# Sliding-window attention and a squared-ReLU FFN on one core: the first block's casts and copies are dealt out anew, w_in is read in 2 KB rows, more pieces get staging homes, and the first stores are issued later

## The chip, the core and the metric

The kernel runs on one core of a Trainium2 chip. The metric is the device time of one execution in microseconds; the time before is the median of three runs. In this text PE is TensorE, DVE is VectorE, ACT is ScalarE, POOL is GpSimd, and SP is SyncE, which only issues DMAs here.

## What is computed

Eight batches of causal attention with a window of 64 positions, 8 heads of 64, 576 positions; then an FFN over all 4608 tokens.

```python
batch, n_heads, seq, head_dim = (8, 8, 576, 64)
rel = pos[:, None] - pos[None, :]
mask = (rel >= 0) & (rel < 64)
attn = softmax(where(mask, q @ k.T / sqrt(64), -1e9))       # per batch and head
x = (attn @ v).transpose(0, 2, 1, 3).reshape(4608, 512)
h = np.maximum(x @ w_in, 0.0)                               # w_in 512 x 2048
out = (h * h) @ w_out                                       # w_out 2048 x 512
```

## The kernel before

The tokens are worked on in nine blocks of 512: block g below 8 is the first 512 positions of batch g, and the ninth collects the last 64 positions of all batches. In the code g0, g1, g2, g3 are the first four. A block's 8 heads are four pairs `hp`. All matrix work is in fp16; the inputs are fp32 and come in by DMA as 256 KB pieces of 128x512 (`load_qk_pair`, `load_v_pair` for the first three blocks, `load_part` from block 3 on).

The steps of one block are small functions. `cast_qk_pair` and `cast_v_pair` turn a piece to fp16; `shift_v_pair` writes v once more, moved by 64 rows (`v_od`), in two halves. `T` transposes q and k of a pair on PE (eight 128x128 transposes) and copies them from PSUM. `add_mask` puts the mask into PSUM with two matmuls, `Sc` adds the scores (16 small matmuls) and takes the exponential on ACT. `AV` multiplies with v, `N` normalises on DVE, `X` transposes the result on PE and copies it into `xT`. `F1` is x @ w_in for 128 hidden columns (four matmuls over c, L358), then ReLU on DVE (L361) and the square on ACT (L362); `F1_open` (L374) does the first of the four matmuls early. `F2` is the second product in quarters (L394), scaled on ACT into `osb`, of which there are five buffers. From block 1's F2 on, products of sums of weights and of activations (`T_sum` into `wsum`, `S_sum` into `hsum`) replace part of the matmuls. `busy` issues matmuls whose result nobody reads.

The order of the instructions on every engine is written out by hand (`tc.manual_schedule()`), and each engine works its own list in order; a step waits only for its operands and for the buffer that it writes. SP issues nearly all DMAs in program order, each one waiting for the DMA eight before it. From block 3 on the q and k of a block are transposed by DMAs on SP (`transpose_part`), four for q and four for k, each behind POOL's cast. The 9 blocks are staggered: while block g's F2 runs, block g+1's F1 and block g+2's attention are woven in.

Staging: a loaded fp32 piece lies in one of ten `stp` buffers unless `homes` names a place for it. `hsum` and `wsum` are 8 places of 128x512 fp32 each; they first hold v of block 0, w_in and w_out, then (hsum) the first eight pieces of block 2, and later the sums. The list `to_store` collects output stores; they are issued on SP when the next F2 reaches its quarter 1.

w_in is loaded as eight pieces of 512 KB. In the first four each row read is 256 columns, 1 KB, and a piece holds all four c of these columns; in the last four a row is 512 columns, 2 KB, and a piece holds two c. POOL casts each piece in two casts.

Of the kernel before, what the change touches and what calls it, by code (L numbers as in the profile page):

```python
# [8 lines left out]
FP32 = mybir.dt.float32  # L9
FP16 = mybir.dt.float16  # L10
AF = mybir.ActivationFunctionType
# [4 lines left out]
def kernel(  # L16
# [17 lines left out]
    P = 128  # L34
# [81 lines left out]
    def copy(engine, out, in_):  # L116
        if engine is nc.scalar:
            engine.activation(out=out, in_=in_, func=AF.Copy, scale=1.0)  # L118
        else:
            engine.tensor_copy(out=out, in_=in_)  # L120
# [3 lines left out]
    w_out_sb = const.tile([P, FFC, DM], FP16, name="w_out_sb")  # L124

    def load_w_in(i):
        if i < 2:
            if i == 0:
                st["w_in"] = h2pool.tile([P, 4, DMC, 256], FP32, name="w_st", tag="h2")
            for half in range(2):  # L130
                cols = slice(i * 512 + half * 256, i * 512 + half * 256 + 256)
                nc.sync.dma_start(
                    out=st["w_in"][:, 2 * i + half, :, :],
                    in_=moe_w_in[:, cols].rearrange("(c p) f -> p c f", p=P))
            return
        for c in range(0, DMC, 2):
            to = wsum[:, 4 * (i - 2) + c:4 * (i - 2) + c + 2, :]
            st["w_in", i, c], st["w_in", i, c + 1] = to[:, 0, :], to[:, 1, :]
            nc.sync.dma_start(
                out=to, in_=moe_w_in[c * P:(c + 2) * P, i * 512:(i + 1) * 512].rearrange("(c p) f -> p c f", p=P))  # L140

    def cast_w_in(i, c, engine):
        if i < 2:
            half, c = c // 2, 2 * (c % 2)
            copy(engine, w_in_sb[:, c:c + 2, i * 512 + half * 256:i * 512 + half * 256 + 256],
                 st["w_in"][:, 2 * i + half, c:c + 2, :])
            return
        copy(engine, w_in_sb[:, c, i * 512:(i + 1) * 512], st["w_in", i, c][:])

    def load_w_out(f):  # L150
# [33 lines left out]
    def cast_qk_pair(g, what, hp, engine):  # L184
        t = p16p.tile([P, 512], FP16, name=f"{what}16", tag=f"{what}16")
        p16[what, g, hp] = t
        copy(engine, t[:].rearrange("p (i h d) -> p h i d", i=4, h=2),
             st[what, g, hp][:].rearrange("p (h i d) -> p h i d", i=4, h=2))

    def cast_v_pair(g, hp, engine):  # L190
        copy(engine, ev[g, 0][:, :, pair(hp), 0:D].rearrange("p c h d -> p h c d"),
             st["v", g, hp][:].rearrange("p (h c d) -> p h c d", h=2, c=4))
# [55 lines left out]
    def T(g, hp, pool=ps_tr, tag="tr", engine=nc.scalar, own=None):  # L248

        qkt = apool.tile([P, 2, 512], FP16, name="qk", tag="qk")  # L250
        if own is not None:
            tr = at_ps[own][:, 0, :].bitcast(FP16).rearrange("p (a b) -> p a b", a=2)
        else:
            tr = pool.tile([P, 2, 512], FP16, name="tr", tag=tag)
        for a, what in enumerate("qk"):
            for i in range(4):
                nc.tensor.transpose(out=tr[:, a, i * P:(i + 1) * P],  # L257
                                    in_=p16[what, g, hp][:, i * P:(i + 1) * P], identity=ident[:])
        copy(engine, qkt[:].rearrange("r a (p i) -> r a p i", i=4),
             tr[:].rearrange("r a (i p) -> r a p i", i=4))  # L260
        qT[g, hp, "unit"], kT[g, hp, "unit"] = qkt[:, 0, :], qkt[:, 1, :]
# [3 lines left out]
    def add_mask(g, hp, apart=False, i=0):  # L265

        if apart:
            sc = [ps_f1.tile([P, 512], FP32, name="sc1", tag="f1")[:] for _ in range(2)]
        else:
            sc = [at_ps[i][:, hh, :] for hh in range(2)]  # L270
        added[g, hp] = sc
        for hh in range(2):
            nc.tensor.matmul(sc[hh], ident[:], maskb[:, 0, :], start=True, stop=False)
# [116 lines left out]
    def F2(g, ts, quarter, pool, tag, into=None):  # L390
        if quarter == 0:
            f2[g, ts] = into if into is not None else pool.tile([P, 512], FP32, name="ops", tag=tag)
        for f in range(4 * quarter, 4 * quarter + 4):
            nc.tensor.matmul(f2[g, ts][:], h2[g][:, f, ts * P:(ts + 1) * P], w_out_sb[:, f, :],  # L394
                             start=(f == 0), stop=(f == FFC - 1))
        if quarter == 3:
            osb = opool.tile([P, DM], FP32, name="osb", tag="osb", bufs=5)
            nc.scalar.activation(out=osb[:], in_=f2[g, ts][:], func=AF.Copy, scale=OUT_SCALE)
            to_store.append(lambda: store(g, ts, osb))
        if quarter == 1:  # L400
            while to_store:
                to_store.pop(0)()

# [215 lines left out]
    with tc.manual_schedule():  # L619
# [7 lines left out]
        for hp in range(HP):  # L627
# [2 lines left out]
                load_v_pair(g0, 0)  # L630
            load_qk_pair(g0, "q", hp)
            load_qk_pair(g0, "k", hp, nc.scalar)
        nc.scalar.activation(out=warm[:], in_=warm[:], func=AF.Exp)
        for hp in range(1, HP):
            load_v_pair(g0, hp)
        for i in range(4):
# [2 lines left out]

        new_v(g0)  # L640
        dve, pool, act = nc.vector, nc.gpsimd, nc.scalar
        for hp in range(3):
            cast_qk_pair(g0, "q", hp, dve)
            cast_qk_pair(g0, "k", hp, dve)
        cast_v_pair(g0, 0, pool)
        cast_qk_pair(g0, "q", 3, pool)
        busy(24, wide=False)
        T(g0, 0)
        busy(1)
        add_mask(g0, 0)  # L650
        Sc(g0, 0)
        T(g0, 1)
        busy(1)
        add_mask(g0, 1, i=1)
        T(g0, 2, ps_f1, "f1", engine=dve)
        cast_qk_pair(g0, "k", 3, dve)
        Sc(g0, 1, i=1)
        add_mask(g0, 2)
        busy(1)
        Sc(g0, 2)  # L660
        T(g0, 3, engine=dve)
        for hp in range(HP):
            shift_v_pair(g0, hp)
        cast_v_pair(g0, 1, act)
        busy(3)
        add_mask(g0, 3, True)
        AV(g0, 0)
        N(g0, 0)
        Sc(g0, 3, True)
        for hp in range(2, HP):  # L670
            cast_v_pair(g0, hp, act)
        busy(1)
        AV(g0, 1, 0)
        N(g0, 1)
        X(g0, 0)
        busy(2)
        AV(g0, 2)
        N(g0, 2)
        X(g0, 1, act, ps_f2, "f2")
        AV(g0, 3, 0)  # L680
        N(g0, 3)
# [44 lines left out]
                cast_v_pair(g1, hp, nc.gpsimd)  # L726
            shift_v_pair(g1, hp, parts=(0, 1) if hp < 3 else (0,))
        new_v(g2)
        for i, key in enumerate([(w, g2, hp) for hp in range(HP) for w in "qkv"][:8]):
            homes[key] = hsum[:, i, :]  # L730
        for hp in range(HP):
            load_qk_pair(g2, "q", hp)
            load_qk_pair(g2, "k", hp)
# [35 lines left out]
        def A(g, hp, i=1):  # L769
            AV(g, hp, i)  # L770
            N(g, hp)
# [11 lines left out]
        cast_v_pair(g1, 2, nc.scalar); cast_v_pair(g1, 3, nc.scalar)  # L783
        shift_v_pair(g1, 3, nc.scalar, (1,))
        A(g1, 0, 0); F(1, second); M(g1, 3)
        A(g1, 1, 1); F(1, second)
        A(g1, 2, 0); X(g1, 0); A(g1, 3, 1); F(1, second)
        X(g1, 1, nc.scalar, *in_f1); X(g1, 2, nc.vector)
        for f in range(2):
            F1_open(g1, f, *(in_f1, in_f2)[f], upto=2)  # L790
        for f in range(2):
            F1_open(g1, f)
        X(g1, 3, nc.vector, *in_f1); T(g2, 0)
        for _ in range(8):
            next_part()
        F(3, first)
# [129 lines left out]
```

## The time and the profile before

| | us |
|---|---|
| median of 3 runs (295.95 to 297.1) | 296.46 |
| the profiled execution's own time | 295.8 |
| its span in the profile | 294.1 |
| PE busy | 285.6 |
| DVE busy | 224.7 |
| ACT busy | 177.6 |
| POOL busy | 125.2 |

Busy times are sums over the span; an engine that waits for a semaphore is idle. The profile covers one execution of the program, and its times are counted from the start of the span. HBM read is 38.80 MB and written 9.44 MB. A line number names the line of the kernel before; L118 and L120 are the helper `copy` (ACT, and DVE or POOL), so there the tile tells which step it is.

### The profile page before, as it was taken

To read this page: it belongs to the slowest core of one execution; us is meant where nothing else is said; L and a number is where in the kernel's file an instruction comes from. 1 tells how busy PE (TensorE), PEld (TensorE's weight loads), DVE (VectorE), ACT (ScalarE), POOL (GpSimd) and SP (SyncE) were. 2 spreads that over 40 slices of the span, in tenths; PEclk is the share of its full clock that TensorE was granted. 3 is DMA by queue.
4 is the path that set the end of the run, shared out by engine and by line. 5 is a ranking of instruction groups with operands and counts; after the bars stand their busy time and mean duration, and the time that the engine had idled before them with its cause. 6 is when DMAs were issued, how large, how long until landed. Compare 5 with 4: busy or idle time off the path is not lost.

```text
span 294.1 us, 7511 instructions
## 1 busy us (share of the span) xinstructions
PE 285.6 (97%) x2953; PEld 185.0 (63%) x2953; DVE 224.7 (76%) x395; ACT 177.6 (60%) x308; POOL 125.2 (43%) x215
## 2 busy tenths in 40 slices
PE   6999999999999999999999999999999999999994
PEld 4544445555445466667666766666666666888883
DVE  5677629498866887878769877887798889878781
ACT  3767747688366556565665566556564655587821
POOL 4769739953384347239526632913333000000002
PEclk9999999999999999999999999999999999999999
DMA  7999999999999997999899999899997023202025
GB/s 236 314 333 393 406 276 272 309 202 185 161 260 179 185 215 148 205 185 238 170 193 212 223 184 234 169 192 210 206 215 203 2 38 92 92 1 74 0 74 143
DMA packets 143651, 56.07 MB, mean 191 GB/s; under 512 B 127712, under 2 KB 136160, under 8 KB 143616
## 3 DMA queue, kind: packets, MB, share of 16 engines
q1 hardware_dynamic: 142144, 53.95, 86.1%
q10 hardware_dynamic: 1328, 1.25, 1.3%
q0 software_dynamic: 144, 0.39, 0.6%
q8 instruction: 23, 0.38, 0.6%
q14 instruction: 12, 0.10, 0.1%
HBM read 38.80 MB, written 9.44 MB: 164 GB/s over the span
## 4 chain that ended last, share of the span: by engine, by line
PE 93%; ACT 3%; DMA 1%; DVE 1%; issue 0%; ACTq 0%; DVEq 0%
PE hps L358 37%; PE chain L446 14%; PE side L446 12%; PE ops L394 5%; PE at L318 4%; PE at L288 4%; PE at L480 4%; PE side L394 2%; PE chain L394 2%; PE more L446 2%; PE at L344 2%; DMA st_k<-in_k_dram 1%; PE at L446 1%; PE tr L257 1%; ACT qk L118 1%; PE hps L374 1%
## 5 line engine op out<-in xcount | busy, mean ns | idle before, releaser
L362 ACT ACTIVATE h<-hr 128x512 f16<-128x512 f32 x128 | 80.0, 630 | 78.9 <-DVE hr L361 78.4
L358 PE MATMUL hps<-xT,w_in_sb 128*128 128x512 f16 x496 | 122.4, 379 | 0.2
L361 DVE TENSOR_SCALAR hr<-hps 128x512 f32<-128x512 f32 x127 | 85.8, 686 | 31.0 <-PE hps L358 28.5
L358 PEld LDWEIGHTS <-w_in_sb 128*128 128x128 f16 x500 | 46.7, 98 | 42.4 <-issue 1.4
L446 PEld LDWEIGHTS <-hsum 128*128 128x128 f16 x448 | 43.0, 98 | 11.8 <-DVE hsum L422 0.2
L120 POOL CAST v_ev<-st_v 128x512 f16<-128x512 f32 x31 | 22.6, 730 | 42.9 <-DMA st_v<-in_v_dram 42.9
L446 PEld LDWEIGHTS <-h 128*128 128x128 f16 x336 | 32.6, 98 | 8.4 <-issue 0.4
L120 POOL CAST k<-st_k 128x512 f16<-128x512 f32 x33 | 21.0, 638 | 37.8 <-DMA st_k<-in_k_dram 36.3
L295 ACT ACTIVATE pm<-at 128x1024 f16<-128x1024 f32 x35 | 34.1, 1014 | 1.4 <-PE at L288 1.3
L387 POOL DMA_DIRECT2D out_dram<-osb x3 | 1.8, 594 | 63.4 <-ACT osb L562 62.0
L302 DVE TENSOR_TENSOR pm<-pm,mask 128x1024 f16<-128x1024 f16 x32 | 24.5, 775 | 2.1 <-ACT pm L295 2.1
L328 DVE TENSOR_TENSOR xs<-at,rden 128x512 f16<-128x512 f32 x36 | 24.9, 692 | 1.2
L446 PE MATMUL chain<-wsum,hsum 128*128 128x256 f16 x192 | 24.9, 273 | 0.0
L422 DVE TENSOR_TENSOR hsum<-h 128x1024 f16<-128x1024 f16 x28 | 20.9, 747 | 5.1 <-ACT h L362 5.0
L233 POOL CAST v_od<-st_v 64x512 f16<-64x512 f32 x30 | 22.2, 742 | 1.6
L120 POOL CAST q<-st_q 128x512 f16<-128x512 f32 x28 | 18.7, 692 | 6.5 <-DMA st_q<-in_q_dram 3.1
L394 PEld LDWEIGHTS <-h 128*128 128x128 f16 x128 | 11.5, 97 | 12.2
L318 PEld LDWEIGHTS <-pm 128*64 128x64 f16 x576 | 11.2, 110 | 7.0 <-issue 2.8
L118 ACT ACTIVATE xT<-at 128x512 f16<-128x512 f16 x22 | 12.8, 586 | 4.0 <-PE at L344 2.7
L394 PE MATMUL ops<-w_out_sb,h 128*128 128x512 f16 x64 | 14.8, 380 | 0.0
L318 PE MATMUL at<-v_ev,pm 128*64 128x65 f16 x384 | 13.9, 197 | 0.2 <-ACT v_ev L118 0.2
L562 ACT ACTIVATE osb<-chain 128x256 f32<-128x256 f32 x36 | 13.4, 371 | 0.3 <-PE chain L446 0.3
(118 smaller groups left out, 384.4 us busy)
## 6 DMA issues: line engine op xcount, KB each, us to landing
st_k<-in_k_dram SPq DMA_DIRECT2D x33, 256.0 KB, 3.8
out_dram<-osb SPq DMA_DIRECT2D x32, 256.0 KB, 3.0
st_q<-in_q_dram SPq DMA_DIRECT2D x29, 256.0 KB, 5.2
st_v<-in_v_dram SPq DMA_DIRECT2D x28, 256.0 KB, 4.4
w_st<-in_moe_w_in_dram SPq DMA_DIRECT2D x4, 512.0 KB, 6.6
wsum<-in_moe_w_in_dram SPq DMA_DIRECT2D x4, 512.0 KB, 9.0
hsum<-in_moe_w_out_dram SPq DMA_DIRECT2D x4, 512.0 KB, 8.0
wsum<-in_moe_w_out_dram SPq DMA_DIRECT2D x4, 512.0 KB, 9.7
```

What stands on the lines that cost most here:

```text
L120: engine.tensor_copy(out=out, in_=in_)
L233: nc.gpsimd.tensor_copy(out=od[g][to:to + 64, m, :, 0:D], in_=st["v", g, c][of:of + 64, :].rearrange("p (h d) -> p h d", h=H))
L295: nc.scalar.activation(out=p[:, hh, :] if apart else p[:], in_=sc[hh] if apart else both[:], func=AF.Exp, scale=1.0 / float(D) ** 0.5)
L302: nc.vector.tensor_tensor(out=p[:], in0=p[:], in1=m.unsqueeze(1).broadcast_to([P, 2, 512]), op=ALU.min)
L318: nc.tensor.matmul(a[jj * 64:(jj + 1) * 64, hh, jp * VW:jp * VW + D + 1], pm[g, hp][:, hh, j * 64:(j + 1) * 64], vsel, start=True, stop=True)
L328: nc.vector.tensor_tensor(out=x[:].rearrange("p j h d -> p h j d"), in0=a[:, :, :, 0:D], in1=rden[:].unsqueeze(3).broadcast_to([P, 2, 4, D ...
L358: nc.tensor.matmul(hps[:], w_in_sb[:, c, f * P:(f + 1) * P], xT[g][:, c, :], start=(c == 0), stop=(c == DMC - 1))
L361: nc.vector.tensor_scalar(out=hr[:], in0=hps[:], scalar1=0.0, scalar2=None, op0=ALU.max)
L362: nc.scalar.activation(out=h2[g][:, f, :], in_=hr[:], func=AF.Square)
L394: nc.tensor.matmul(f2[g, ts][:], h2[g][:, f, ts * P:(ts + 1) * P], w_out_sb[:, f, :], start=(f == 0), stop=(f == FFC - 1))
L422: (engine or nc.vector).tensor_tensor(out=out, in0=a, in1=b, op=op)
L446: nc.tensor.matmul(to, a[:, f, :], b[:, f, :], start=start and f == 0, stop=f == HF - 1, skip_group_check=True)
```

## The change

1. `load_w_in` and `cast_w_in`: all eight pieces are read in 2 KB rows, two c and 512 columns each.
2. On ACT the table load (the first exponential, `warm`) is issued after two of the four k loads of block 0, not after all four.
3. In block 0 the casts of q1, q2 and k2 go from DVE to POOL, those of v1 and v2 from ACT to DVE (v3 stays on ACT), one `shift_v_pair` from POOL to DVE, the copy of `T(g0, 1)` from ACT to DVE and that of `T(g0, 3)` from DVE to ACT. `T(g0, 1)` comes ahead of `Sc(g0, 0)`, `AV(g0, 0)` and `AV(g0, 1)` ahead of the mask and scores of pair 3, `X(g0, 0)` behind `AV(g0, 2)`. Eight of nine wide `busy` matmuls are left out.
4. In block 1, X of pairs 0 and 1 comes one product earlier, X of pair 3 ahead of the second `F1_open`s.
5. Block 2's last four pieces and block 3's four q pieces are staged in `wsum` instead of `stp`.
6. Block 0's stores are no longer issued within its own F2; they are issued in block 1's F2, on SP behind the loads and transposes of block 3.

```diff
     def load_w_in(i):
-        if i < 2:
-            if i == 0:
-                st["w_in"] = h2pool.tile([P, 4, DMC, 256], FP32, name="w_st", tag="h2")
-            for half in range(2):
-                cols = slice(i * 512 + half * 256, i * 512 + half * 256 + 256)
-                nc.sync.dma_start(
-                    out=st["w_in"][:, 2 * i + half, :, :],
-                    in_=moe_w_in[:, cols].rearrange("(c p) f -> p c f", p=P))
-            return
+        if i == 0:
+            st["w_in"] = h2pool.tile([P, 2, DMC, 512], FP32, name="w_st", tag="h2")
         for c in range(0, DMC, 2):
-            to = wsum[:, 4 * (i - 2) + c:4 * (i - 2) + c + 2, :]
+            to = st["w_in"][:, i, c:c + 2, :] if i < 2 else wsum[:, 4 * (i - 2) + c:4 * (i - 2) + c + 2, :]
...
-        if quarter == 1:
+        if quarter == 1 and g > 0:
             while to_store:
                 to_store.pop(0)()
...
-        nc.scalar.activation(out=warm[:], in_=warm[:], func=AF.Exp)
+            if hp == 1:
+                nc.scalar.activation(out=warm[:], in_=warm[:], func=AF.Exp)
...
-        for hp in range(3):
-            cast_qk_pair(g0, "q", hp, dve)
-            cast_qk_pair(g0, "k", hp, dve)
+        cast_qk_pair(g0, "q", 0, dve)
+        cast_qk_pair(g0, "k", 0, dve)
+        cast_qk_pair(g0, "q", 1, pool)
+        cast_qk_pair(g0, "k", 1, dve)
+        cast_qk_pair(g0, "q", 2, pool)
+        cast_qk_pair(g0, "k", 2, pool)
         cast_v_pair(g0, 0, pool)
         cast_qk_pair(g0, "q", 3, pool)
         busy(24, wide=False)
         T(g0, 0)
         busy(1)
         add_mask(g0, 0)
+        T(g0, 1, ps_f1, "f1", engine=dve)
         Sc(g0, 0)
-        T(g0, 1)
-        busy(1)
         add_mask(g0, 1, i=1)
+        shift_v_pair(g0, 0, dve)
         T(g0, 2, ps_f1, "f1", engine=dve)
+        Sc(g0, 1, i=1)
         cast_qk_pair(g0, "k", 3, dve)
-        Sc(g0, 1, i=1)
         add_mask(g0, 2)
-        busy(1)
         Sc(g0, 2)
-        T(g0, 3, engine=dve)
-        for hp in range(HP):
+        T(g0, 3)
+        for hp in range(1, HP):
             shift_v_pair(g0, hp)
-        cast_v_pair(g0, 1, act)
-        busy(3)
-        add_mask(g0, 3, True)
+        cast_v_pair(g0, 1, dve)
+        cast_v_pair(g0, 2, dve)
         AV(g0, 0)
         N(g0, 0)
-        Sc(g0, 3, True)
-        for hp in range(2, HP):
-            cast_v_pair(g0, hp, act)
-        busy(1)
         AV(g0, 1, 0)
         N(g0, 1)
-        X(g0, 0)
-        busy(2)
+        cast_v_pair(g0, 3, act)
+        add_mask(g0, 3, True)
+        Sc(g0, 3, True)
         AV(g0, 2)
         N(g0, 2)
+        X(g0, 0)
         X(g0, 1, act, ps_f2, "f2")
...
-        for i, key in enumerate([(w, g2, hp) for hp in range(HP) for w in "qkv"][:8]):
-            homes[key] = hsum[:, i, :]
+        for i, key in enumerate([(w, g2, hp) for hp in range(HP) for w in "qkv"] + [("q", g3, c) for c in range(4)]):
+            homes[key] = hsum[:, i, :] if i < 8 else wsum[:, 2 * (i % 4) + (1 if i < 12 else 0), :]
...
-        A(g1, 1, 1); F(1, second)
-        A(g1, 2, 0); X(g1, 0); A(g1, 3, 1); F(1, second)
-        X(g1, 1, nc.scalar, *in_f1); X(g1, 2, nc.vector)
+        A(g1, 1, 1); F(1, second); X(g1, 0)
+        A(g1, 2, 0); X(g1, 1, nc.scalar, *in_f1); A(g1, 3, 1); F(1, second)
+        X(g1, 2, nc.vector)
         for f in range(2):
             F1_open(g1, f, *(in_f1, in_f2)[f], upto=2)
+        X(g1, 3, nc.vector, *in_f1)
         for f in range(2):
             F1_open(g1, f)
-        X(g1, 3, nc.vector, *in_f1); T(g2, 0)
+        T(g2, 0)
```

More of the change, by code (lines that the diff above doesn't have):

```diff
@@ L142, in cast_w_in @@
     def cast_w_in(i, c, engine):
[L143 to L147, printed above, removed]
         copy(engine, w_in_sb[:, c, i * 512:(i + 1) * 512], st["w_in", i, c][:])
```

## The prediction

> **What bounds the kernel now.** I read the page's busy shares first.
>
> ```profile
> PE 285.6 (97%) x2953; PEld 185.0 (63%) x2953; DVE 224.7 (76%) x395; ACT 177.6 (60%) x308; POOL 125.2 (43%) x215
> ```
>
> TensorE is busy 285.6 of 294.1 us. An edit on other engines can only win where TensorE waits, so next come the windows: PE busy time is the second number, the granted clock and DMA stand at the end.
>
> ```profile
> 15.00:20.00 5.00, 4.43 (x57) 2.52 (x56) 3.24 (x8) 2.51 (x5) 3.51 (x6) 1.00 0.97 306
> 50.00:55.00 5.00, 4.42 (x50) 2.67 (x50) 2.39 (x6) 2.16 (x4) 4.72 (x9) 1.00 1.08 298
> 100.00:150.00 50.00, 50.00 (x539) 32.92 (x539) 41.92 (x73) 28.61 (x52) 26.76 (x40) 1.00 1.06 196
> ```
>
> From 100 us on nothing is to be had: what is won before then must reach the end as an earlier start of this solid stretch. What is to be had lies ahead of the first dense F1 stretch and at 50 to 55 us. The chain of waits shows who holds TensorE there (start, us, what):
>
> ```profile
> 4.97 1.28 ACT L633
> ...
> 6.26 0.20 ACT warm L633
> 6.47 0.92 ACT qk L118
> ...
> 7.88 1.02 ACT pm L295
> ...
> 14.90 1.04 ACT v_ev L118 x2
> 15.94 0.98 ACT xT L118 x2
> ...
> 18.46 0.44 DVE xT L120
> 18.90 0.04 issue
> 18.94 9.24 PE hps L358 x42
> ```
>
> Until 17 us the chain runs through ScalarE: the table load, two qk copies, exponentials, two v casts, two xT copies. The F1 stream starts at 18.94, when the last xT quarter is copied, and TensorE then runs 42 matmuls in 9.24 us (0.22 each). So ScalarE's queue ahead of block 0's F1 is the bound, and the dummy matmuls that go are not on it.
>
> **The change, part by part.** Rows for the head, from the timeline:
>
> ```profile
> 5.12 0.63 PE L257 MATMUL tr<-ident,k 128*128 128x128 f16 x4
> 5.66 0.43 DVE L120 CAST q<-st_q 128x512 f16<-128x512 f32 x1 [0.66 <-DMA st_q<-in_q_dram]
> 5.98 0.95 PE L273 MATMUL at<-maskb,ident 128*128 128x512 f16 x2
> 7.57 0.43 DVE L120 CAST k<-st_k 128x512 f16<-128x512 f32 x1
> 8.45 0.61 POOL L120 CAST v_ev<-hsum 128x512 f16<-128x512 f32 x1 [4.29 <-DMA hsum<-in_v_dram]
> 9.60 1.22 DVE L120 COPY qk<-tr 128x1024 f16<-128x1024 f16 x1 [1.61 <-PE tr L257]
> 10.31 4.61 POOL L120 CAST v_od<-hsum 64x384 f16<-64x384 f32 x8
> 15.46 1.17 POOL L120 CAST w_in_sb<-w_st 128x512 f16<-128x512 f32 x2 [0.54 <-DMA w_st<-in_moe_w_in_dram]
> 16.81 1.17 POOL L120 CAST w_in_sb<-w_st 128x512 f16<-128x512 f32 x2 [0.18 <-DMA w_st<-in_moe_w_in_dram]
> 20.48 1.17 POOL L120 CAST w_in_sb<-w_st 128x512 f16<-128x512 f32 x2 [0.61 <-DMA w_st<-in_moe_w_in_dram]
> 21.83 1.17 POOL L120 CAST w_in_sb<-wsum 128x512 f16<-128x512 f32 x2 [0.18 <-DMA wsum<-in_moe_w_in_dram]
> 25.78 1.17 POOL L120 CAST w_in_sb<-wsum 128x512 f16<-128x512 f32 x2 [0.15 <-DMA wsum<-in_moe_w_in_dram]
> ```
>
> *Table load ahead of the third and fourth k load.* ScalarE is free when pair 0's transposes end (5.12 + 0.63 = 5.75), so the first qk copy runs 5.8 to 6.7 instead of 6.47 to 7.39. The third k load is issued about 1.5 us later (1.28 + 0.20), which costs nothing if its queue is still busy with the two k loads before it; its old arrival is about 7.5 (DVE's cast at 7.57). If it isn't hidden, k2 comes up to 1.5 us late, and with it T(g0, 2).
>
> *T(g0, 1) ahead of Sc(g0, 0), copied by DVE.* After the masks (5.98 + 0.95 = 6.93, the last of it drain) TensorE does pair 1's transposes: the q cast is now GpSimd's, 5.66 + 0.61 = 6.27, in time. DVE's copy takes 1.22, about 7.6 to 8.8, and scores 0 follow at 7.3 to 7.7: their exponential ends at 8.7 instead of 8.90. GpSimd then has q2 and k2 (0.61 each, to 8.4 with the arrival at 7.5), v0 and q3 (to 9.0 and 10.3; their users, T(g0, 3) and AV(g0, 0), wait longer for ScalarE and DVE), and six shifts instead of eight ahead of the w_in casts, done by about 13.8, before the first piece lands. Scores 1 start at 8.8, exponential to 10.3.
>
> *Two shift halves on DVE ahead of T(g0, 2)'s copy.* A 64x384 shift on DVE has no row. Bounds: 0.43, its own cast of more columns, and GpSimd's 4.61 / 8 = 0.58. I take 0.35 each as fewer columns, 0.3 to 0.58 for the range. They delay the copy: 8.8 + 0.7 + 1.22 = 10.7. Scores 2 at 10.7, exponential 11.15 to 12.2. Little is won up to here.
>
> *ScalarE's rest.* Behind it remain the pair 3 copy (0.92, to 13.1), one v cast instead of three (14.90's row: 1.04 for two, so 0.52; to 13.6), exponential 3 (1.02; to 14.65) and the xT copies 0 and 1 (0.98; to 15.6, was 16.92). The other two v casts are on DVE at 0.43 each, behind k3's, ahead of N(g0, 0), ending by 12.0, while TensorE still waits for the exponential 2. AV(g0, 3), its normalisation, transpose and DVE's 0.44 copy give xT's last quarter at about 17.4.
>
> *w_in in 2 KB rows.* The casts begin when a 512 KB piece lands. In 1 KB rows three pieces take 20.48 - 15.46 = 5.02, 1.67 each; in 2 KB rows 25.78 - 21.83 = 3.95 for three, 1.32 each. If all eight are at 1.32 the first two land some 0.4 and 0.7 earlier (15.0, 16.1) and everything behind them 1.4 earlier. Against that, f = 0 now needs two pieces rather than one (all four c of the first 512 columns): 16.1 + 1.17 = 17.3. So F1 starts at 17.4 to 17.5 by both limits: **1.5 us** earlier. Range: 1.0 if the first piece comes no earlier, 2.0 if TensorE's side were early too.
>
> The Trainium skill, DMA: Bandwidth & Descriptors, section Specifications, puts the transfer size for line rate at 512 B or more; by that, 1 KB rows are as good as 2 KB rows, and the total would be rival 1's. The rows above (1.67 against 1.32) disagree with it for these column slices.
>
> *The eight wide dummy matmuls that go* cost nothing and win nothing: TensorE waits around them.
>
> *X of block 1 earlier.* The 50 to 55 window has 0.58 idle, and the list of PE's waits names its largest part:
>
> ```profile
> PE hps L374 <- ACT xT L118: 0.5, 1, 0.5
> ```
>
> After the change X(g1, 0) and X(g1, 1) are transposed before the last attention products, their copies lie beside F2 matmuls, and the transposes of g2 follow the four F1 openings. At least the 0.58 goes, at most 1.0 (half of each drain too): I take **0.8**.
>
> *Staging homes and stores.* They win nothing by themselves, but decide whether the 2.3 us survive, because block 3's scores are due exactly when their last operand lands:
>
> ```profile
> 54.49 1.54 SPq L383 DMA_DIRECT2D out_dram<-osb  x3
> 62.14 0.61 POOL L120 CAST q<-st_q 128x512 f16<-128x512 f32 x1 [0.90 <-PE hps L358]
> 79.26 1.22 SPq L242 DMA_TRANSPOSE kT<-k  x1
> DMA to landing us min/median/max: 3.5/3.5/3.5
> 80.31 0.60 ACT L398 ACTIVATE osb<-side 128x512 f32<-128x512 f32 x1 [0.27 <-PE side L394]
> 80.57 0.53 SPq L383 DMA_DIRECT2D out_dram<-osb  x1
> 81.90 0.63 ACT L362 ACTIVATE h<-hr 128x512 f16<-128x512 f32 x1 [0.99 <-DVE hr L361]
> 82.79 0.64 PE L288 MATMUL at<-qT,kT 64*128 64x64 f16 x32
> ```
>
> The last transposing DMA of block 3 is issued at 79.26 and lands 3.5 later, at 82.8; Sc(g3) starts at 82.79. There is no slack: without an earlier SP queue every us won in the head stops here. Three stores (1.54 of issue, 768 KB of a busy DMA) now leave SP's way, the stp buffers are no longer shared by eight more pieces, and all weights land 1.4 earlier. I put T(q) of block 3 at about 60.5 instead of 63, the last landing at 77 to 80, against 80.5 needed.
>
> Sum: 1.5 + 0.8 = 2.3. The profiled execution took 295.8 (span 294.1), which becomes 293.5. The runs' median, 0.66 above that execution, is 296.46, so I predict **294.2**; its own range is 293.4 to 295.0 (gains of 3.0 and 1.5). A measurement can tell about 0.5%, 1.5 us, from no change.
>
> **Rivals.**
> 1. *2 KB rows bring nothing* (0.13). Pieces land as before, the second at 16.8, the fourth at 20.5. F1 starts after 16.81 + 1.17 = 18.0, and f = 4 needs the fourth piece's casts at 21.65, while TensorE would be there at 20.8. The head's gain shrinks to 0.1, with 0.8 from X: about 295.5. For it: f = 0 needs twice the weights. Against: 1.67 against 1.32.
> 2. *Block 3 stays late* (0.12). If the last kT lands at 81.5 to 82.8 rather than 80.5, 1 to 2.3 are lost: 295.2 to 296.5. For it: SP must still issue the same loads and transposes in order, each behind a GpSimd cast. Against: the stores gone.
> 3. *ScalarE blocked by a store, slower* (0.08). There are five osb buffers; the sixth (the 80.31 row) needs the first store landed. That store is now issued behind block 3's last transpose. If SP gets there no earlier than now (80.57, the stores' first landing some 3 us later, an estimate near the 3.5 above), ScalarE stands from 80.3 to 83.6, and squares and block 3's exponentials wait behind it. Its 0.99 of idle absorbs a part, at most 2.3 go to TensorE, and block 3 has eaten the gain as in rival 2: 297.3, to 298.5 if SP is later still. It decides from a landing about 2 us after osb is due. If SP is early, as I expect, the wait is under 1.5 and hidden.
> 4. *The clock falls back, slower* (0.05). Without the dummies the head has pauses.
>
> ```profile
> 288.89 1.04 PE L446 MATMUL at<-wsum,h 128*128 128x256 f16 x8
> 290.00:294.10 4.10, 0.00 (x0) 0.00 (x0) 0.00 (x0) 0.35 (x1) 0.33 (x1) 0.91 0.46 125
> ```
>
> After the last matmul (289.93) the granted clock is 0.91 over 4.1 us: at half speed that is 0.74 us, so it fell at 293.36, 3.4 us after the last matmul. My longest pause is about 1.5 us (scores 1 to scores 2). If it fell, F1's first 5 us would run at 0.43 per matmul (the two masks at 5.98, 0.95 with drain) instead of 0.22, 2.4 lost, and the head's scores and products about 1.4 more: 298.0. The Trainium skill, TensorE: Matmul & The Clock Gate, Part 1, says the clock halves after an idle window of about 3.4 us; by that rule, the trace agrees.
>
> **How the numbers follow.** Forecast 0.62, rivals 0.13, 0.12, 0.08, 0.05. Faster by over 0.5% is below 295.0: nearly all of the forecast and a little of rival 1 or 2, 0.63. Slower is above 297.9: half of rival 3 and rival 4, 0.09. The rest is 0.28. The range 293.4 to 296.6 leaves out rivals 3 and 4 and a twentieth below.
>
> **What would show it.** The first long hps L358 piece at 17.4 to 17.6; a DVE T(g0, 1) copy near 7.6; w_in cast pairs 1.3 apart from the first on; no PE wait for ACT xT at 50; Sc(g3) near 80.5 without a wait, and stores issued at 75 to 78. Wrong: a PE wait for POOL w_in casts at 18 to 21, for kT near 80, an ACT wait for DMA out_dram at 78 to 82, or matmuls at 0.43 after 8 us.

## The result, and the profile after

The changed kernel takes 295.46 us (median of 16 executions, 295.04 to 296.63); the kernel before took 296.47 on the same chip (16 executions, 295.52 to 297.94). The ratio is 0.9966 with a 95% interval of [0.9951, 0.9981]: 1.0 us won, where 2.3 were forecast; 295.46 lies above the 293.4 to 295.0 that the forecast gave itself. The profiled execution took 296.1 us (span 294.3), one of the slowest of its sixteen, while the one of before (295.8) was among the faster: the two traces show where time goes, the medians how much.

In the page of the profile, TensorE is busy 1.6 us less (eight instructions fewer, the wide dummies); DVE and GpSimd have more to do, ScalarE less:

```profile
PE 284.0 (96%) x2945; PEld 183.9 (62%) x2945; DVE 225.8 (77%) x396; ACT 176.8 (60%) x306; POOL 128.8 (44%) x216
```

The same three windows as before (PE busy is the second number):

```profile
15.00:20.00 5.00, 3.89 (x42) 2.19 (x43) 2.51 (x7) 2.36 (x5) 3.07 (x6) 1.00 1.00 349
50.00:55.00 5.00, 4.97 (x66) 3.04 (x65) 2.93 (x8) 2.31 (x4) 4.66 (x10) 1.00 1.07 296
100.00:150.00 50.00, 50.00 (x539) 32.87 (x539) 41.47 (x73) 28.70 (x52) 25.59 (x40) 1.00 1.08 199
```

At 50 to 55 us the idle time is gone (4.42 became 4.97). In the head (the time before block 0's F1) it has grown: 3.89 busy where 4.43 were. The chain of waits says why:

```profile
11.73 6.29 DMA w_st<-in_moe_w_in_dram
18.02 0.05 issue
18.08 0.62 POOL w_in_sb L120
18.70 0.05 issue
18.75 0.61 PE hps L362 x2
19.35 9.26 PE hps L346 x42
...
70.00 0.61 DVE hr L349
70.61 0.04 issue
70.66 1.02 PE hps L346 x4
...
82.92 0.57 PE at L276 x32
```

(All line numbers of the steps are 12 lower than before: L346 is F1, L349 its ReLU, L362 the early F1 matmuls, L276 the scores.) The last thing that F1 waits for is no longer ScalarE or DVE, but w_in's second piece: it lands at 18.02, GpSimd casts it, and the 42 F1 matmuls start at 19.35, 0.4 later than before instead of 1.5 earlier. TensorE's waits agree, and ScalarE's show the store of rival 3:

```profile
PE hps L362 <- POOL w_in_sb L120: 0.9, 1, 0.9
PE at L276 <- DVE qk L120: 0.9, 1, 0.9
...
PE hps L346 <- DVE hr L349: 0.3, 1, 0.3
...
ACT osb L386 <- DMA out_dram<-osb: 1.4, 1, 1.4
```

Rows from the timelines of the engines that were rearranged, each row with its engine:

```profile
5.50 1.02 ACT L118 ACTIVATE qk<-tr 128x1024 f16<-128x1024 f16 x1 [2.13 <-PE tr L245]
7.35 1.22 DVE L120 COPY qk<-tr 128x1024 f16<-128x1024 f16 x1 [0.49 <-PE tr L245]
9.37 1.09 DVE L120 CAST v_od<-hsum 64x384 f16<-64x384 f32 x2 [0.79 <-DMA hsum<-in_v_dram]
10.49 1.22 DVE L120 COPY qk<-tr 128x1024 f16<-128x1024 f16 x1
11.97 1.38 DVE L120 CAST v_ev<-hsum 128x512 f16<-128x512 f32 x2
11.77 0.41 PE L276 MATMUL at<-qk 64*128 64x64 f16 x16 [0.88 <-DVE qk L120]
15.69 1.67 ACT L118 ACTIVATE xT<-xtr 128x512 f16<-128x512 f16 x3
15.48 1.17 POOL L120 CAST w_in_sb<-w_st 128x512 f16<-128x512 f32 x2
18.08 1.17 POOL L120 CAST w_in_sb<-w_st 128x512 f16<-128x512 f32 x2 [1.43 <-DMA w_st<-in_moe_w_in_dram]
19.62 2.49 POOL L120 CAST w_in_sb<-w_st 128x512 f16<-128x512 f32 x4 [0.38 <-DMA w_st<-in_moe_w_in_dram]
17.90 0.42 DVE L120 COPY xT<-xtr 128x512 f16<-128x512 f16 x1 [0.63 <-PE xtr L332]
77.56 1.22 SPq L230 DMA_TRANSPOSE kT<-k  x1
78.83 2.03 SPq L371 DMA_DIRECT2D out_dram<-osb  x4
81.47 0.60 ACT L386 ACTIVATE osb<-side 128x512 f32<-128x512 f32 x1 [1.37 <-DMA out_dram<-osb]
```

DVE has xT's last quarter ready at 18.32 (17.90 and 0.42), so without the wait for the cast the stream would have begun about 0.9 us earlier. The second piece is cast 2.6 us after the first (15.48, 18.08); the forecast had 1.1 for that.

### The profile page after: what moved, and what is told of

Its sections match the earlier page's. It is cut to its first block, busy times and chain, and to the rows that moved or that the text cites. A ratio compares the mean times of both kernels' runs of the same rounds, so it can differ in the third digit from the quotient of the medians.

```text
span 294.3 us, 7488 instructions
## 1 busy us (share of the span) xinstructions
PE 284.0 (96%) x2945; PEld 183.9 (62%) x2945; DVE 225.8 (77%) x396; ACT 176.8 (60%) x306; POOL 128.8 (44%) x216
## 4 chain that ended last, share of the span: by engine, by line
PE 91%; DMA 4%; SPq 1%; DVE 1%; ACT 1%; issue 0%; POOL 0%; DVEq 0%
PE hps L346 36%; PE chain L434 14%; PE side L434 12%; PE ops L382 5%; PE at L306 4%; PE at L468 4%; PE at L276 3%; PE side L382 2%; PE chain L382 2%; DMA hsum<-in_v_dram 2%; DMA w_st<-in_moe_w_in_dram 2%; PE more L434 2%; PE at L332 2%; PE at L434 1%; PE tr L245 1%; SPq L168 1%
## 5 line engine op out<-in xcount | busy, mean ns | idle before, releaser
L346 PE MATMUL hps<-xT,w_in_sb 128*128 128x512 f16 x496 | 122.5, 379 | 0.3 <-DVE hr L349 0.3
L349 DVE TENSOR_SCALAR hr<-hps 128x512 f32<-128x512 f32 x127 | 85.7, 686 | 32.0 <-PE hps L346 29.7
L346 PEld LDWEIGHTS <-w_in_sb 128*128 128x128 f16 x500 | 46.6, 98 | 42.6 <-issue 1.2
L120 POOL CAST k<-st_k 128x512 f16<-128x512 f32 x33 | 23.0, 701 | 34.2 <-DMA st_k<-in_k_dram 31.6
L290 DVE TENSOR_TENSOR pm<-pm,mask 128x1024 f16<-128x1024 f16 x32 | 23.9, 759 | 1.9 <-ACT pm L283 1.9
L221 POOL CAST v_od<-st_v 64x512 f16<-64x512 f32 x30 | 21.3, 711 | 1.6
L120 POOL CAST q<-st_q 128x512 f16<-128x512 f32 x25 | 17.5, 721 | 6.6 <-DMA st_q<-in_q_dram 6.3
```

The costliest lines, as they stand in the source:

```text
L221: nc.gpsimd.tensor_copy(out=od[g][to:to + 64, m, :, 0:D], in_=st["v", g, c][of:of + 64, :].rearrange("p (h d) -> p h d", h=H))
L290: nc.vector.tensor_tensor(out=p[:], in0=p[:], in1=m.unsqueeze(1).broadcast_to([P, 2, 512]), op=ALU.min)
L346: nc.tensor.matmul(hps[:], w_in_sb[:, c, f * P:(f + 1) * P], xT[g][:, c, :], start=(c == 0), stop=(c == DMC - 1))
L349: nc.vector.tensor_scalar(out=hr[:], in0=hps[:], scalar1=0.0, scalar2=None, op0=ALU.max)
```

## The experiments

Sixteen runs, in four groups; kernels of a group ran on one chip beside the kernel before (its medians: 296.11 to 296.3). "The change without 2 KB rows" is the changed kernel with w_in's first four pieces read in 1 KB rows as before.

### First group: is the result stable, and which part gives what

The kernel before and the changed kernel again, unedited.

> The kernel before once more, to see how far its own head moves between executions. Both theories: ratio 1.00 within 0.15%. Theory A: F1 at 18.7 to 19.2 again, q2 at about 7.1. Theory B: F1 and the landing of q2 differ by 0.5 us or more from the first profile (18.94 and 7.10).

Measured 0.9997 [0.9981, 1.0013] (ratio to the kernel before, with its 95% interval), median 296.18. In this execution block 3's last kT lands at 80.86 and its scores start at 82.88: two microseconds of slack, where the first profile had none. "No slack" was chance of one execution.

> The changed kernel once more. Its first profile (296.1, a slow one of runs with median 295.46) has F1's stream starting at 19.30 against 18.94 before, because q2 of block 0 landed at 8.3 instead of 7.1 and the second w_in piece at 18.0. Theory A (the loads are late in every run, by the change): q2's cast again after 8.2, F1 again at 19.0 or later, time 295.2 to 295.8, and all of the 1.0 won comes from X of block 1. Theory B (chance of that one execution): q2's cast at 7.1 to 7.6, F1 at 17.4 to 18.4.

Measured 0.9975 [0.9956, 0.9994], 295.39. TensorE again waits for w_in's cast, 1.2 us in all.

The changed kernel with the table load behind all four k loads again:

```diff
-            if hp == 1:
-                nc.scalar.activation(out=warm[:], in_=warm[:], func=AF.Exp)
+        nc.scalar.activation(out=warm[:], in_=warm[:], func=AF.Exp)
```

> The changed kernel with the table load behind all four k loads, as before. Theory C (the table load between the k loads makes q2 and k2 late): q2 lands at 7.1 again, w_in pieces about 0.9 earlier than in the changed kernel, and the time is the same or 0.3 to 0.8 lower in spite of ScalarE's later start. Theories A and B without it: q2 as in the changed kernel's repeat; first qk copy at 6.4 instead of 5.5, which costs 0 to 0.6 us.

Measured 0.9994 [0.9976, 1.0012], 296.2: 0.8 above the changed kernel of the same group, though the intervals touch. q2 of block 0, which landed late in the first profile after (8.34 against 7.10 before), lands at 7.23 here and at 7.13 in the repeat of the changed kernel: the move of the table load does not make it late in every execution. Over all profiles it landed later than 7.5 in five of twelve with the early load and in none of six with the late one; whether the move makes it more frequent stays open.

The kernel before with part 4 (X of block 1) alone:

```diff
-        A(g1, 1, 1); F(1, second)
-        A(g1, 2, 0); X(g1, 0); A(g1, 3, 1); F(1, second)
-        X(g1, 1, nc.scalar, *in_f1); X(g1, 2, nc.vector)
+        A(g1, 1, 1); F(1, second); X(g1, 0)
+        A(g1, 2, 0); X(g1, 1, nc.scalar, *in_f1); A(g1, 3, 1); F(1, second)
+        X(g1, 2, nc.vector)
...
```

> The kernel before with only the new places of X in block 1 (part 4 of the change). My prediction's term: 0.8 less, ratio 0.9973. By the one pair of profiles: 0.5 less (0.9982), since F1 of block 1 went from 0.36 late to 0.12 early. If block 3's scores have no slack, as the prediction says of the kernel before, a wait of PE near 82 us eats most of it: 0.9995 to 1.0.

Measured 0.9975 [0.9959, 0.999], 295.38: 0.75 us won by this part (0.3 to 1.2 by the interval), 0.8 forecast. The window:

```profile
50.00:55.00 5.00, 4.80 (x62) 2.77 (x62) 3.80 (x9) 2.86 (x6) 4.72 (x9) 1.00 1.11 312
```

This execution's head ran late (F1 starts at 20.61; the last section says why), so the window does not hold quite the same work as before. From F1's start to block 3's scores it takes 63.43 us, where the kernel before took 63.85: in the trace the part wins 0.4.

### Second group: the other parts

The kernel before with 2 KB rows alone (part 1):

```diff
-        if i < 2:
-            ...
-                    in_=moe_w_in[:, cols].rearrange("(c p) f -> p c f", p=P))
-            return
+        if i == 0:
+            st["w_in"] = h2pool.tile([P, 2, DMC, 512], FP32, name="w_st", tag="h2")
         for c in range(0, DMC, 2):
+            to = st["w_in"][:, i, c:c + 2, :] if i < 2 else wsum[...]
```

> The kernel before with only w_in in 2 KB rows (part 1). My prediction's step: pieces 1.32 apart from the first on, F1 no later than before, time 0 to 0.7 lower (0.9976 to 1.0). The theory of its failure: the second piece lands at 17.6 to 18.0, as in both profiles of the changed kernel, and F1, which now needs two pieces, starts at 18.9 to 19.3 and waits for POOL's w_in casts: 0 to 0.4 higher (1.0 to 1.0015).

Measured 1.0003 [0.9979, 1.0026], 296.79. Here F1's last operand is xT, as before, so the rows neither win nor lose by more than the interval. Of the 1.4 us by which "all eight at 1.32" was to bring everything forward, nothing is seen in the time, and the last piece is cast at 25.7, against 25.8 in the first profile before. The trace cannot be laid beside the first one in more than this, since its clock rose late: the transposes that begin at 8.19 still run at half speed, those at 10.13 at full speed (before: full speed from 6.7), and F1 starts at 20.12.

```profile
8.19 0.61 PE L245 MATMUL tr<-ident,q 128*128 128x128 f16 x4
10.13 0.39 PE L245 MATMUL tr<-ident,q 128*128 128x128 f16 x4
```

The changed kernel with 1 KB rows, the other way round (`load_w_in` and `cast_w_in` as before):

```diff
+        if i < 2:
+            ...
+                    in_=moe_w_in[:, cols].rearrange("(c p) f -> p c f", p=P))
+            return
-        if i == 0:
-            st["w_in"] = h2pool.tile([P, 2, DMC, 512], FP32, name="w_st", tag="h2")
```

> The changed kernel with w_in read as before, 1 KB rows in the first four pieces, so that the first F1s need one piece. Theory of the failed step (the second piece holds F1 back): F1 starts at 17.3 to 17.8, PE waits for a later cast at 18 to 20 at most 0.8, and the time is 0.4 to 1.2 below the changed kernel: 294.3 to 295.0, ratio to before 0.993 to 0.9965. By my prediction (2 KB rows bring weights earlier) it is 0 to 1 above the changed kernel.

Measured 0.994 [0.9921, 0.9958], 294.73: better than both kernels.

The changed kernel without parts 5 and 6 (staging and stores as before):

```diff
-        if quarter == 1 and g > 0:
+        if quarter == 1:
...
-        for i, key in enumerate([...] + [("q", g3, c) for c in range(4)]):
+        for i, key in enumerate([...][:8]):
```

> The changed kernel without parts 5 and 6: block 2's and 3's pieces back in stp, the first stores back within block 0's F2. My prediction's rival 2: Sc of block 3 has no slack without them, so a PE wait shows at 80 to 83 and the whole gain is lost (0.9985 to 1.0). The repeat of the kernel before had its last kT of block 3 at 80.9 against scores at 82.9, so there were 2 us of slack in that run: then the time is that of the changed kernel (0.9965 to 0.998).

Measured 0.9967 [0.9943, 0.999], 295.35: the same as with them. Its last kT is issued at 77.78, its scores start at 82.96:

```profile
77.78 1.22 SPq L230 DMA_TRANSPOSE kT<-k  x1
...
82.96 0.64 PE L276 MATMUL at<-qT,kT 64*128 64x64 f16 x32
```

Against 77.56 and 82.85 with the two parts, nothing moved. In this trace TensorE's largest wait is again for w_in:

```profile
PE hps L362 <- POOL w_in_sb L120: 1.5, 1, 1.5
```

The changed kernel with the eight wide dummies put back, spread over five places of block 0:

```diff
+        busy(1)
...
+        busy(1)
...
+        busy(3)
...
+        busy(1)
...
+        busy(2)
```

> The changed kernel with the eight wide dummy matmuls put back at places of the same kind. My prediction: no difference (ratio 0.9965 to 0.9975, as the changed kernel). Theory of the clock: in one profile of a kernel with the old head the granted clock was 0.5 for 3.4 us from 7.8 on; if pauses in the head cause that, the dummies take the slow tail away (no run over 0.7 us above the median). Theory of the instruction fetch: PE's next 16 KB of instructions come at 11 instead of 14.7, ahead of the second w_in piece, which then lands at 16.5 to 17, and F1 starts 0.7 earlier.

Measured 0.9975 [0.9949, 1.0001], 295.71: no difference from the changed kernel that the intervals show. The profiled execution, 294.59, is the fastest of its twelve: in it the second piece of w_in lands at 16.31 and F1 starts at 18.13. The same holds for the kernel with the late table load (294.86, the fastest of its twelve; 16.78 and 18.06). In the other four profiles that have the new head and 2 KB rows the second piece lands at 17.8 to 18.4, F1 starts at 19.1 to 19.7, and the executions take 295.4 to 296.1. So with one row size and nearly one order, the time goes with the landing of the second piece.

### Third group: the head by itself, and two attempts at more

The kernel before with parts 2 and 3 alone, rows of 1 KB (the change's lines of block 0, of which these are the first):

```diff
+            if hp == 1:
+                nc.scalar.activation(out=warm[:], in_=warm[:], func=AF.Exp)
-        nc.scalar.activation(out=warm[:], in_=warm[:], func=AF.Exp)
...
+        T(g0, 1, ps_f1, "f1", engine=dve)
         Sc(g0, 0)
-        T(g0, 1)
...
```

> The kernel before with only block 0's casts, copies, order and the earlier table load (parts 2 and 3), w_in in 1 KB rows. By subtraction (the changed kernel with 1 KB rows won 1.6, X alone 0.75, homes and stores nothing) it should win 0.6 to 1.0: ratio 0.9966 to 0.998, F1 at 17.8 to 18.1. My prediction's head term without the rows was 1.5 (0.995). If the 1.6 came from something else together, below 0.3.

Measured 0.997 [0.9951, 0.9989], 295.55: the head's order wins 0.55 us by the medians and 0.9 by the ratio, where the 2 KB rows are absent. In its profile, too, the clock rose late (transposes at full speed only from 9.4), so its F1 start, 18.44, is not the order's best.

The change without 2 KB rows, DVE's shift moved behind `T(g0, 2)` and k3's cast:

```diff
-        shift_v_pair(g0, 0, dve)
         T(g0, 2, ps_f1, "f1", engine=dve)
         Sc(g0, 1, i=1)
         cast_qk_pair(g0, "k", 3, dve)
+        shift_v_pair(g0, 0, dve)
```

> The changed kernel with 1 KB rows, and with the two shift halves of pair 0 on DVE behind the copy of T(g0, 2) and k3's cast. In its profiles they took 1.1 to 1.5 for two, not the 0.7 that my prediction took, and PE stood 0.9 to 1.6 before the scores of pair 2 for the copy behind them. Theory D (this DVE queue is what F1 now waits for): scores 2 come 1.0 earlier, F1 at 17.0 to 17.4, and 0.3 to 0.8 are won against the 1 KB variant's 294.7: 293.9 to 294.4 (ratio 0.9915 to 0.993). Theory E (the weights hold F1 anyway, second piece at 17): scores 2 earlier, F1's third group still at 18.2, 0 to 0.2 won.

Measured 0.9963 [0.9943, 0.9983], 295.13. TensorE's wait for the copy of pair 2 shrinks (0.52 against 0.99 in the second run without the move), but nothing of it reaches the end: the time is no better than the 294.73 without the move in the second group. Miss.

The same two kernels (the change without 2 KB rows, and that with the late shift) with the dummies back, by the same five lines as above:

> The changed kernel with 1 KB rows and the eight dummies put back. In ten profiles PE's 16 KB instruction fetch came either before 13.6, and the first two w_in pieces landed 1.3 to 1.7 apart, or at 14.2 to 14.8, and they landed 2.7 to 3.2 apart. Theory F (the fetch holds up a piece, and the dummies move the fetch): fetch at 11 to 12, pieces 1.3 to 1.7 apart, but F1 gains at most 0.3 since it needs one piece at first: 294.3 to 294.8. If the fetch has nothing to do with the pieces: early fetch and pieces 2.5 or more apart. Time without effect: 294.5 to 295.0.

> Both of the last two edits together. If theory E holds alone (weights limit once the shift is moved) and theory F holds, the two together win more than either: 293.6 to 294.2, F1's stream without a wait for POOL's w_in casts. If neither: 294.4 to 295.0.

Measured 0.9973 [0.9954, 0.9992], 295.67, and 0.9971 [0.995, 0.9993], 295.47: the dummies make neither better. The first is slower than the same kernel without dummies in the second and fourth groups (294.73 and 294.42), and its trace shows a reason: from the scores of pair 2 (10.95) to xT's last transposes (17.46) it takes 6.51 us, without the dummies 5.80 (11.15 to 16.95). Once F1 does not wait for w_in, the dummies lie in TensorE's way. But the kernel without them was not run on this chip, and the three kernels of this group that have the change's order and 1 KB rows (0.9963 to 0.9973) are no faster than the changed kernel (0.9966 to 0.9975): here the rows' price does not show.

### Fourth group: are the 2 KB rows the cause, and by which way

Still open was whether the changed kernel and the one with 1 KB rows differ on one chip, and if so, whether it is because F1's first columns need two pieces. The two, unedited:

> The changed kernel once more, beside the next two on the same chip. All theories: 0.9965 to 0.9975 of the kernel before. Its second w_in piece lands 2.6 to 3.2 us behind the first and PE waits about 1 us for POOL's w_in casts.

> The changed kernel with the first four w_in pieces in 1 KB rows, on the same chip as the changed kernel. If the 2 KB rows cost the head its gain (the present theory): 0.993 to 0.9955, 0.4 to 0.9 us below the changed kernel. If the 0.73 us between the earlier two calls was the chip's: 0.9965 to 0.9975, as the changed kernel.

Measured 0.9967 [0.9947, 0.9986], 295.55, for the changed kernel, and 0.9932 [0.9905, 0.9959], 294.42, with 1 KB rows (only 6 executions): 1.1 us apart on the same chip by the medians. The two intervals overlap by 0.0012, but the same kernel gave 0.994 [0.9921, 0.9958] in the second group, so that the difference stands on two runs. The timeline with 1 KB rows:

```profile
15.41 1.17 POOL L120 CAST w_in_sb<-w_st 128x512 f16<-128x512 f32 x2 [0.69 <-DMA w_st<-in_moe_w_in_dram]
17.57 1.17 POOL L120 CAST w_in_sb<-w_st 128x512 f16<-128x512 f32 x2 [0.99 <-DMA w_st<-in_moe_w_in_dram]
...
15.06 1.67 ACT L118 ACTIVATE xT<-xtr 128x512 f16<-128x512 f16 x3
17.38 0.42 DVE L120 COPY xT<-xtr 128x512 f16<-128x512 f16 x1 [0.73 <-PE xtr L344]
17.85 3.49 PE L358 MATMUL hps<-xT,w_in_sb 128*128 128x512 f16 x15
```

The second piece is late here too (17.57), but F1 does not need it yet: it starts at 17.85, right behind xT's last quarter, 1.09 earlier than before.

The changed kernel with only w_in's first megabyte (pieces 1 and 2) in 1 KB rows:

```diff
+        if i == 0:
+            halves = st["w_in"][:, 0, :, :].rearrange("p c f -> p (c f)").rearrange("p (h c f) -> p h c f", h=2, c=DMC)
+            for half in range(2):
+                nc.sync.dma_start(
+                    out=halves[:, half, :, :],
+                    in_=moe_w_in[:, half * 256:half * 256 + 256].rearrange("(c p) f -> p c f", p=P))
+            return
...
```

> The changed kernel, where only w_in's first 1 MB (pieces 1 and 2) is read in 1 KB rows, all else in 2 KB rows. If what costs is that the first F1 needs two pieces: as the kernel with 1 KB rows or up to 0.3 us better, 0.9925 to 0.9955, F1's first matmuls right after the first piece's casts at 16.5 to 18 us. If the cost lies in the rows or the pieces 3 and 4: as the changed kernel, 0.9965 to 0.9975.

Measured 0.9953 [0.9932, 0.9975], 294.93. Its timeline:

```profile
14.50 1.17 POOL L120 CAST w_in_sb<-w_st 128x512 f16<-128x512 f32 x2 [0.24 <-DMA w_st<-in_moe_w_in_dram]
17.17 1.17 POOL L120 CAST w_in_sb<-w_st 128x512 f16<-128x512 f32 x2 [1.50 <-DMA w_st<-in_moe_w_in_dram]
...
17.55 2.75 PE L357 MATMUL hps<-xT,w_in_sb 128*128 128x512 f16 x12
20.49 0.39 PE L357 MATMUL hps<-xT,w_in_sb 128*128 128x512 f16 x1 [0.18 <-POOL w_in_sb L120]
```

Although the second piece lands 2.7 us after the first, F1 starts at 17.55. So in the traces it is the need for two pieces at the start that costs. From f = 4 on, where pieces 3 and 4 hold two c each, it waits again, and its list of waits has two for a cast, 0.4 us in all; by the medians this kernel lies between the other two, by the intervals it is apart from neither.

The kernel before without the eight wide dummies:

```diff
-        busy(1)
...
-        busy(1)
...
-        busy(3)
...
-        busy(1)
...
-        busy(2)
```

> The kernel before without the eight wide dummy matmuls that the change leaves out, nothing else changed. The prediction's term: 0, ratio 1.000. Theory that PE's instruction fetch sets how w_in's second piece lands: the fetch moves from 11 to 14 us or later, the second piece lands 2.6 us or more behind the first, 0 to 0.3 us worse. Theory that the dummies guard the clock: the head has stretches of 3.4 us with PE busy at 0.6 or less, and some executions are 1.2 to 1.7 us longer.

Measured 1.0 [0.9983, 1.0018], 296.77. No gain, as the prediction had it, and no loss that the interval shows. But in 7 of its 12 executions the mean granted clock (TensorE's, as a share of full speed) is 0.994 (296.71 to 297.76 us), against 2 of 25 at 0.992 or less and none at 0.994 of the kernel before beside it. One window of 3.41 us at half speed takes 0.006 off the mean, so this is one fallen window; its own profile has none, so that it falls in the head is inferred. In the old order, then, the dummies seem to fill pauses in which the clock falls now and then. In the changed kernel, without dummies, 4 of 40 executions have a mean of 0.994 or less, with the dummies back 1 of 12: there they guard nothing that shows. PE's fetch of instructions, which the transfers show as a queue of its own (16 KB each; that it is PE's is inferred), came at 12.7 and the second piece landed 1.5 us after the first: leaving out the dummies does not by itself bring the 14 or later and the 2.6 that the fetch theory expected.

## Why the prediction was wrong, point by point

**The step that failed: w_in in 2 KB rows.** The prediction put the second piece at 16.1, its cast's end at 17.3, and had F1 start at 17.4 to 17.5 "by both limits". It had taken 1.32 us per piece from the last pieces' casts and applied it from the first. Measured in the changed kernel: first piece 15.36, second 18.02 (17.82 and 17.88 in the repeats), third 19.57. The 1.3 us can be relied on only from the second or third piece on, in either row size: with 1 KB rows the casts start at 15.41, 17.57, 19.06, 20.43, with 2 KB rows at 15.48, 18.08, then two pairs in a row from 19.62. The last piece is no earlier either: its casts start at 25.2 to 26.1 in nine of ten profiles with 1 KB rows at the start, at 25.0 to 26.5 with 2 KB rows. The 1.67 against 1.32 on which the prediction rested was nearly all the place in the stream, not the row: the fourth piece lands 1.37 to 1.43 after the third in nine of ten profiles with 1 KB rows and 1.30 to 1.32 after it in all eight with 2 KB rows, so that 0.1 a piece is left for the rows. The Trainium skill's rule (DMA: Bandwidth & Descriptors, Specifications: 512 B or more for line rate), which the prediction set aside for these rows, agrees with the runs but for this 0.1. What remains of the part is its price, which the prediction had named: f = 0 needs two pieces instead of one. Together with the late second piece it made GpSimd's cast the last wait, 0.9 us in the first profile, and cost 1.1 us by the medians (294.42 against 295.55 on one chip; the kernels of the third group do not show this price). Rival 1, at 0.13, was the closest: 295.5 forecast, 295.46 measured, with its stated mechanism (F1 behind the second piece's cast), though the second piece was later than its 16.8 and the wait for f = 4 was not the one that counted. That its number fits to 0.04 is luck: it had F1 0.1 earlier than before, and in the three profiles F1 starts 0.2 to 0.4 later.

**The head's order: right in its mechanism, too large by 0.4.** ScalarE's first copy starts at 5.50 (5.8 forecast) and DVE's copy of T(g0, 1) at 7.35 (7.6). With the rows out of the way F1 starts at 17.85 (18.04 in the other profile) instead of 17.4 to 17.5: 1.1 (0.9) won of 1.5. The terms that were mis-sized are DVE's: the two shift halves took 1.09 (0.55 each; 0.35 taken, 0.58 the upper bound) and 1.50 in another execution with 1 KB rows, beyond the bound; they also began late, behind v0's landing, for which the sum had no wait. The two v casts took 1.38, 0.69 each instead of 0.43. So scores 2 started at 11.77, not 10.7. ScalarE's first two xT copies ended about 0.5 later than the 15.6 of the sum in the kernel with 1 KB rows (15.06 plus two thirds of 1.67) and at 16.8 in the first profile. GpSimd casts at the same time; that this is what slows DVE was not tried.

**X of block 1: right in its mechanism, and in its size as far as the interval tells.** 0.75 alone by the medians, 0.4 in the one trace, 0.8 forecast, and the wait for ACT xT is gone from the list of TensorE's waits.

**The dummies: as forecast for the changed kernel.** The cover named (TensorE waits around them) holds while F1 waits for w_in; with 1 KB rows the trace has them in the way. That in the old order they also seem to hold up the clock was missed.

**Homes and stores: no effect, and the slack was misread.** The stores are issued at 78.8 (75 to 78 forecast), the last kT lands at 80.81 (77 to 80), the scores start without a wait for it. But the same kernel without these parts is as fast. The prediction rested on one execution in which the landing and the scores fell together; in the next one they were 2 us apart.

**Rival 3** took place in small: ScalarE waits 1.37 us for the first store's landing, hidden, as the prediction argued for a wait under 1.5. **Rival 2** did not occur. **Rival 4**: no fall shows in the first profile after, one shows in the second repeat; its condition, a pause of 3.4 us, was wrong (last section). The prediction had read the 3.4 from one profile, as the time from the last matmul to the fall; over all eighteen profiles that time is 2.1 to 4.9.

**The sum.** X 0.75 and the head 0.55 to 0.9 make 1.3 to 1.65; the two runs with 1 KB rows give 1.6 and 1.85 by the medians, short of the 2.3 of the sum. Less the 1.1 of the rows, 0.2 to 0.75 would remain; 0.7 to 1.0 were measured, so the three do not add up better than to some 0.4 us. In several traces of the new head F1 waits 0.2 to 0.4 for DVE's ReLU later on (at 70 us in the first one), which gives a part of the gain back.

## What to carry to other kernels

A rate read from the tail of a DMA stream does not hold for its head: for the first consumer, count how many pieces must have landed before it can start, and take the landing of each from its own row. When the waiting engine's queue is shortened, write down the next operand's arrival with the latest landing that the trace supports, not with the one that just fits. Slack of zero in one execution is not a bound: a second execution moved it by 2 us. And before two traces of a head are compared, see when the clock first rose in each: here that was between 4 and 10 us.

## What the runs showed of the hardware

**The clock falls without an idle window.** In three profiles the granted clock fell to 0.5 for one window of 3.41 us in the head. For each, the window before the fall and the one with it: X alone, the late shift, and the changed kernel's second repeat. The fourth pair has no fall: the kernel with only the first megabyte in 1 KB rows.

```profile
4.42:7.83 3.41, 1.56 (x23) 0.84 (x25) 1.98 (x6) 2.40 (x3) 0.00 (x0) 1.00 1.13 339
7.83:11.24 3.41, 3.41 (x39) 2.30 (x33) 0.39 (x2) 1.99 (x2) 1.98 (x4) 0.50 1.19 319
```

```profile
14.31:17.72 3.41, 2.05 (x55) 1.51 (x47) 1.96 (x6) 2.21 (x5) 1.88 (x4) 1.00 1.05 357
17.72:21.13 3.41, 3.41 (x15) 1.73 (x15) 1.25 (x3) 0.96 (x2) 2.66 (x6) 0.50 1.07 382
```

```profile
7.70:11.11 3.41, 2.02 (x38) 1.00 (x38) 3.08 (x5) 1.79 (x2) 2.31 (x5) 1.00 1.20 322
11.11:14.52 3.41, 3.41 (x64) 2.22 (x60) 2.72 (x7) 2.51 (x3) 3.16 (x6) 0.50 1.00 263
```

```profile
8.26:11.67 3.41, 2.04 (x45) 1.26 (x45) 3.33 (x6) 1.65 (x3) 2.21 (x5) 1.00 1.22 306
11.67:15.08 3.41, 3.25 (x84) 2.21 (x82) 3.31 (x8) 3.37 (x6) 2.97 (x7) 1.00 1.03 324
```

TensorE was busy 1.56, 2.05 and 2.02 of 3.41 us, a share of 0.46 to 0.60, with pauses of at most 1.3 us. Of the other windows of these heads that were cut in the same phase, those with 2.09 of 3.41 and more were not followed by a fall, nor were two with as little as 2.04 (the pair above) and 2.06 (the late shift, from 7.48). So the border lies near a share of 0.6, and busy time as the profile counts it does not draw it sharply. The phase differs from execution to execution: the clock first reached 1.0 between 4.1 and 6.8 us in sixteen profiles, and only at 9.4 and 10.0 in two (parts 2 and 3 alone, 2 KB rows alone), where four transposes that take 0.39 us elsewhere took 0.61 to 0.63 until then. So a head with pauses does not have to stand still for 3.4 us to lose the clock, as the prediction assumed with the Trainium skill (TensorE: Matmul & The Clock Gate, Part 1, which names an idle window); a window that was busy for 0.46 to 0.60 was enough here. The first of these executions is 1.7 us above its kernel's median, the second 2.2, the third, whose fall came while the head waited for w_in anyway, 0.1 below.

**One early piece of w_in comes late, and which one varies.** Each is 512 KB, and most land 1.2 to 1.5 us after the one before. But the second landed 1.3 to 1.7 us after the first in some profiles (before 1.42, its repeat 1.42, 2 KB rows alone 1.30, dummies put back 1.30), 2.6 to 3.2 in others (the changed kernel's three 2.66, 2.69 and 2.55, without parts 5 and 6 3.19, X alone 2.94), and in two between; where it is early the third is often late (1.9 in before, 2.1 with the dummies back). It goes closely with the instruction fetch, a transfer of 16 KB that comes once between 10.7 and 15.7 us in every profile: in the eight profiles with the fetch before 13 us the second piece landed 1.3 to 1.7 after the first, in nine of the ten with the fetch from 13.4 on it landed 2.0 to 3.2 after it (the tenth, the late table load: 13.6 and 1.7). With the dummies put back the fetch came at about 11 in three kernels of the new head, and each time the gap was 1.3 to 1.7. That the fetch holds the piece up fits this, but is not shown: nothing was tried that moves the fetch alone, and a late third piece is not explained by it. For the kernel before it is of no account, since F1 waits for xT; for a start that needs two pieces it is 1.3 us or more.
